# Attention's first stage rewritten across four engines: distances by TensorE, exponentials read from PSUM, splits, sums and rebases on GpSimd

## The chip, the cores and the metric

The kernel runs on one core of one Trainium2 chip. The metric is the time of one execution in microseconds (us), taken on the device; of several executions the median counts. A core has five engines with a queue of instructions each: TensorE (PE, with its weight loads listed apart as PEld), VectorE (DVE), ScalarE (ACT), GpSimd (POOL), and SyncE (SP), which issues the DMAs here. Each engine works through its queue strictly in the order written; engines wait for each other by semaphores. Lnnn is line nnn of the kernel that is shown.

## The reference

Windowed attention feeds two feed-forward blocks:

```python
# q, k, v: (2, 8, 768, 64); n_global = 8, n_local = 96
scores = (q @ k.transpose(0, 1, 3, 2)) / np.sqrt(D)
keep = is_global | is_local            # first 8 keys, or 0 <= i - j < 96
dist = np.where(is_global & ~is_local, n_local, np.abs(rel))
slopes = 2.0 ** (-8.0 * (np.arange(H) + 1) / H)      # 2^-1 .. 2^-8
scores = np.where(keep, scores - slopes[:, None, None] * dist, -1e9)
a = np.exp(scores - scores.max(-1)); a = a / (a.sum(-1) + 1e-9)
x = (a @ v) reshaped to 1536 tokens x 512
h = x @ w_in;  g = np.where(h > 0, h, np.exp(np.minimum(h, 0)) - 1);  y = g @ w_out
out = max(y @ w1, y @ w2, y @ w3) @ w_out2
```

The feed-forward weights arrive as 64-bit numbers and are turned into pairs of float32 values (a high and a low part) inside the kernel.

## The kernel before

Attention is cut into 48 steps. A step is (g, hp, t): a group g of 256 tokens, a pair hp of heads, one of the two 128-row halves t of the group. Only the keys that a row block can see are touched: 232 columns, or 128 for the first block of a sequence. Steps 0 to 15 (`first` = 16) give the first 512 tokens; they, with steps 16 and 17, make up the first stage, a loop in `windowed` that is software-pipelined by hand. The order in which the loop calls the helpers is the order of every engine's queue. The other steps are woven into the feed-forward loop `run`, one to a chunk of 128 hidden units; `run` begins when the first stage has issued its last instruction. Its first ACT instruction on a hidden chunk is L525 (`elu_exp`).

One step k in the first stage before the change:

- POOL multiplies the queries of a pair of steps by -2^(head+1)/8 (`scale_queries`, L187), once the DMA of `raw` has landed.
- PE multiplies queries and keys for two heads into two PSUM tiles (`scores_pe`, L217): S0 and S1 in even steps, y0 and y1 in odd ones.
- DVE adds the distances `rel`, scales by 2^-(head+1), writes the values `p` to SBUF and takes their minimum, in one custom instruction with an accumulator read behind it, for each of the two heads (`scores_dve`, L243).
- ACT takes exp(min - p) in place with the row sums as a by-product (`scores_act`, L264), and adds 1e-9 to the sums (`sums`, L226).
- DVE takes the reciprocal (`recip`, L255) and normalizes p (`norm`, L277, one instruction per head), both one step later.
- PE transposes p into a PSUM tile TX, y2 or y3 (`turn_pe`, L287 or L293), two steps after the scores; ACT copies that back to SBUF (`turn_act`, L304).
- PE multiplies with the values (`values_pe`, L316), three steps after the scores; ACT rounds the result to `xh` (`values_high`, L326), and DVE subtracts to get `xl` (`values_low`, L332).

From step 7 on (`CONV`) a generator `convert` puts one piece of weight conversion behind each step. For the chunks c = 0, 1, 2 these are: `c_rebase` (ACT, L404, 128x1024 values), `c_low` (DVE, L408), two `c_word` (DVE, L415, "words" from here on, each with two inputs in SBUF), `c_high` (ACT, L423) and `c_rest` (DVE, L428). In steps 0 and 1 PE also gets two idle matmuls (`fill`, L593), and eight at the start (`warm`). The distances are built once at the start from the two numbers n_global and n_local (`positions`, then `bases`, whose last instruction is L158). Before `run`, two thirds of a first feed-forward product (L505) are issued in steps 16 and 17 and at `run`'s beginning.

Of the kernel before, what the change touches and what calls it, by code (L numbers as in the profile page):

```python
# [23 lines left out]
P = 128  # L24
# [84 lines left out]
class Windowed:  # L109
# [4 lines left out]
    def __init__(self, tc, ctx, io, ps, xy, wt, act):  # L114
        self.nc, self.io, self.ps, self.xy, self.wt, self.act = tc.nc, io, ps, xy, wt, act
        self.const = ctx.enter_context(tc.tile_pool(name="acst", bufs=1))
        self.qk = ctx.enter_context(tc.tile_pool(name="qk", bufs=2))
        self.sm = ctx.enter_context(tc.tile_pool(name="sm", bufs=3))
        self.steps = [
            (g, hp, t) for g in range(NT // GRP) for hp in range(HP) for t in range(2)  # L120
        ]
        self.loaded, self.scaled = 0, set()
        self.qk_t, self.v_t = {}, {}
        self.s_t, self.p_t, self.t_t, self.at_t = {}, {}, {}, {}
        self.xraw = {}

    def positions(self, scratch):

        nc, c = self.nc, self.const
        n = P + WIN  # L130
        rel = c.tile([P, n], F32, name="rel")
        key, neg = scratch[0][:, 0:n], scratch[1][:, 0:n]
        far = 1 << 20
        o = 0
        for num, step, base, cm, kstep, kbase in (
            (P, -1, 0, 1, 1, 0),
            (PREV, -1, PREV, 1, 0, far),
            (G, 0, far, 0, 1, 0),
            (P, -1, 0, 1, 0, far),
        ):  # L140
# [8 lines left out]
        self.base, self.key, self.tmp = rel, key, neg  # L149

    def bases(self, ng, nl, a, b):
# [6 lines left out]
        nc.vector.scalar_tensor_tensor(rel, key, nl, t, op0=ALU.max, op1=ALU.min)  # L158

    def geom(self, s):  # L160

# [20 lines left out]
    def scale_queries(self, p):  # L182
        if p in self.qk_t and p not in self.scaled:
            self.scaled.add(p)
            q = self.qk_t[p][:, 0:GRP]
            c = self.steps[2 * p][1]
            self.nc.gpsimd.tensor_scalar(  # L187
                q, q, self.qsc[:, c:c + 1], 1.0, op0=ALU.mult, op1=ALU.mult
            )

    def load_values(self, k, early=False):

# [7 lines left out]
        )  # L200
        self.v_t[k], self.v_t[k + 1] = v[:, 0], v[:, 1]

    def scores_pe(self, k, tags=("S0", "S1"), m=1):

        if k >= len(self.steps):
            return
        nc = self.nc
        sp = [self.ps.tile([P, 512], F32, tag=a, name=a) for a in tags]
        for s in range(k, k + m):
            t = s % 2  # L210
            _, _, k0, n = self.geom(s)
            o = (s - k) * WIN
            for u in range(2):
                r = slice(u * D, u * D + D)
                kk = slice(GRP + k0, GRP + k0 + n)
                qk = self.qk_t[s // 2]
                nc.tensor.matmul(  # L217
                    sp[u][:, o:o + n], qk[r, t * P:t * P + P], qk[r, kk],
                    start=True, stop=True,
                )  # L220
            self.s_t[s] = [x[:, o:o + n] for x in sp]

    def sums(self, k):
        if k in self.p_t:
            m = self.p_t[k][1]
            self.nc.scalar.activation(m[:, 4:6], m[:, 2:4], AF.Copy, bias=1e-9)  # L226

    def scores_dve(self, k, early=False, other=-1):

        if k not in self.s_t:  # L230
            self.recip(other)
            return
        nc = self.nc
        i, _, _, n = self.geom(k)
        hp = self.steps[k][1]
        sp = self.s_t.pop(k)
        pool, tag = (self.act, "gh") if early and k % 4 > 1 else (self.sm, "p")
        p = pool.tile([P, 512], F32, tag=tag, name="p")
        m = self.sm.tile([P, 8], F32, tag="m", name="m", bufs=4)
        b0 = P if i else 0  # L240
        for u in range(2):
            o = slice(u * WIN, u * WIN + n)
            nc.vector.tensor_tensor_reduce(  # L243
                out=p[:, o], in0=sp[u], in1=self.base[:, b0:b0 + n],
                scale=2.0 ** -(2 * hp + u + 1), scalar=3e38,
                op0=ALU.add, op1=ALU.min, accum_out=m[:, u:u + 1],
            )
            if u == 0:
                self.recip(other)
        self.p_t[k] = p, m  # L250

    def recip(self, k):
        if k in self.p_t:
# [3 lines left out]
    def scores_act(self, k):  # L257
        if k >= len(self.steps):
            return
        n = self.geom(k)[-1]  # L260
        p, m = self.p_t[k]
        for u in range(2):
            o = slice(u * WIN, u * WIN + n)
            self.nc.scalar.activation(  # L264
                p[:, o], p[:, o], AF.Exp, bias=m[:, u:u + 1], scale=-1.0,
                accum_out=m[:, 2 + u:3 + u],
            )

# [49 lines left out]
                    start=c == 0, stop=c == nch - 1,  # L318
                )

    def values_high(self, k, x):

        if k >= 0:
            g, hp, t = self.steps[k]
            o = g * GRP + t * P
            self.nc.scalar.copy(x[0][:, hp, o:o + P], self.t_t[k][0][:, 0:P])  # L326

    def values_low(self, k, x):
        if k >= 0:
            g, hp, t = self.steps[k]  # L330
            o = g * GRP + t * P
            self.nc.vector.tensor_tensor(  # L332
                x[1][:, hp, o:o + P], self.t_t.pop(k)[0][:, 0:P],
                x[0][:, hp, o:o + P].bitcast(F32), op=ALU.subtract,
            )

    def pair_pe(self, k):

# [19 lines left out]
class Feed:  # L358
# [42 lines left out]
    def c_rebase(self, c):  # L401
        for r, _ in self.parts(c):
            a = r[..., 1].bitcast(F32)
            self.nc.scalar.activation(a, a, AF.Copy, scale=2.0 ** -112)  # L404

    def c_low(self, c):
# [442 lines left out]
def windowed(tc, ctx, io, flag):  # L849
# [3 lines left out]
    with tc.manual_schedule():  # L853
# [10 lines left out]
        x = f.split_tiles()  # L864

        def convert():
            f.c_rebase(0)
# [7 lines left out]
            f.c_rebase(1)  # L875
# [9 lines left out]
            f.c_rebase(2)  # L885
# [10 lines left out]
        h = f.ps.tile([P, 512], F32, tag="h", name="h")  # L896
        for k in range(first + 2):
            e = k % 2
            at.load_values(k, True)
            if e == 0:  # L900
                at.load_pair(k // 2 + 3, k < first)
                at.scale_queries(k // 2 + 1)
            if k <= first:
                at.scores_pe(k, (("S0", "S1"), ("y0", "y1"))[e], 1 + (k == first))
# [18 lines left out]
        at.values_pe(first - 1)  # L923
        at.turn_pe(first, "TX")
        at.values_high(first - 1, x)
        at.turn_act(first, nc.scalar.copy)
        at.values_low(first - 1, x)
        at.recip(first + 1)
        at.norm(first + 1)
        next(words, None)  # L930
        f.run(at, first + 2, x, h, lambda: covered(nc, at.const, ng, nl, flag))

# [104 lines left out]
```

## Time and profile before

| | |
|---|---|
| time, 3 runs | 570.61 us median (569.98 to 571.79) |
| span of the profiled execution | 569.0 us |
| PE busy | 549.6 us (97%) |
| DVE busy | 315.4 us (55%) |
| ACT busy | 277.1 us (49%) |
| POOL busy | 78.3 us (14%) |
| first feed-forward ACT instruction (L525), end of the first stage's path | 48.66 us |

The span runs from the first to the last instruction of the profiled execution; what a timed run has beyond it lies ahead of and behind the program (the median of the runs is 1.6 us above this span). Shares of busy time are means over stages that have different limits, so the first stage, the first 48.66 us, has to be read by itself.

### The profile page before, as it was taken

How to read it: one execution, taken by the hardware profiler on the slowest of the kernel's cores; microseconds unless marked ns; L12 is line 12 of the kernel's file. 1: busy time of each engine (PE TensorE's matmuls, PEld its weight loads, DVE VectorE, ACT ScalarE, POOL GpSimd, SP SyncE). 2: the span in 40 equal slices, each digit the busy share in tenths (PEclk: the TensorE clock that was granted, in tenths of full speed). 3: DMA queues.
4: the chain of work that ended last, by engine and by line, in shares of the span. 5: the costliest groups of instructions: out<-in, count | busy, mean ns of one | idle time of the engine just before them, and what ended most of it. 6: DMA issues, size and time to landing. Idle time of an engine off the chain costs nothing. (4 is left out here: it accounts for less than half of the span.)

```text
span 569.0 us, 7586 instructions
## 1 busy us (share of the span) xinstructions
PE 549.6 (97%) x2772; PEld 435.0 (76%) x2772; DVE 315.4 (55%) x684; ACT 277.1 (49%) x622; POOL 78.3 (14%) x87
## 2 busy tenths in 40 slices
PE   8799999999999999999999999999999999999995
PEld 6467777776777777778888888888887888888884
DVE  6987999999745333333466656567754112312112
ACT  5988777777656555554555554524323101311011
POOL 4100222222210000000011222023320000000000
PEclk9969999999999999999999999999999999999999
DMA  8919444532211111010013223122302000010002
GB/s 293 381 45 345 166 168 137 181 122 78 67 36 42 42 41 43 20 55 1 0 38 111 88 98 111 37 75 77 117 29 75 1 1 0 8 67 1 0 1 79
DMA packets 16669, 46.61 MB, mean 82 GB/s; under 512 B 1776, under 2 KB 1776, under 8 KB 16624
## 3 DMA queue, kind: packets, MB, share of 16 engines
q1 hardware_dynamic: 15760, 44.47, 22.8%
q10 hardware_dynamic: 864, 1.57, 0.8%
q8 instruction: 24, 0.39, 0.3%
q14 instruction: 21, 0.17, 0.1%
HBM read 42.90 MB, written 3.15 MB: 81 GB/s over the span
## 5 line engine op out<-in xcount | busy, mean ns | idle before, releaser
L505 PE MATMUL h<-xh,w 128*128 128x512 f32 (+1 forms) x536 | 144.5, 391 | 0.8 <-ACT xh L485 0.8
L505 PEld LDWEIGHTS h<-xh,w 128*128 128x128 f32 x536 | 98.1, 188 | 24.5 <-issue 1.8
L536 PE MATMUL y<-gh,w 128*128 128x512 f32 x384 | 98.6, 399 | 0.0
L512 ACT CAST gh<-e 128x512 fp32r<-128x512 f32 x66 | 41.0, 622 | 101.8 <-DVE e L725 87.4
L536 PEld LDWEIGHTS y<-gh,w 128*128 128x128 f32 x384 | 69.7, 188 | 18.1 <-ACT e L526 1.7
L725 DVE TENSOR_TENSOR e<-S,e 128x512 f32<-128x512 f32 x36 | 24.9, 692 | 103.5 <-PE S L505 100.8
L505 PE MATMUL h<-xl,w 128*128 128x512 f32 (+1 forms) x268 | 81.8, 386 | 0.0
L505 PE MATMUL S<-xh,w 128*128 128x512 f32 x288 | 77.0, 389 | 0.0
L530 DVE SCALAR_TENSOR_TENSOR e<-e,h 128x512 f32<-128x512 f32 x48 | 33.0, 687 | 67.7 <-ACT e L526 67.7
L505 PEld LDWEIGHTS S<-xh,w 128*128 128x128 f32 x288 | 54.1, 188 | 11.2
L525 ACT ACTIVATE e<-h 128x512 f32<-128x512 f32 x48 | 28.7, 597 | 65.2 <-PE h L505 63.0
L462 POOL TENSOR_TENSOR w<-wr,w 128x512 fp32r<-128x512 f32 x24 | 35.4, 1474 | 166.1 <-ACT w L461 166.1
L505 PEld LDWEIGHTS h<-xl,w 128*128 128x128 f32 x268 | 50.0, 188 | 10.3
L517 DVE TENSOR_TENSOR gl<-e,gh 128x512 fp32r<-128x512 f32 x50 | 39.8, 796 | 31.8 <-ACT gh L512 31.6
L264 ACT ACTIVATE p<-p,m 128x232 f32<-128x232 f32 (+1 forms) x96 | 44.8, 469 | 24.4 <-DVE m L243 24.4
L544 PE MATMUL y<-gl,w 128*128 128x512 f32 x192 | 51.5, 390 | 0.0
L415 DVE SCALAR_TENSOR_TENSOR wr<-wr 128x1024 uint32<-128x1024 uint32 (+1 forms) x36 | 49.9, 1395 | 0.8 <-ACT wr L404 0.2
L505 PE MATMUL S<-xl,w 128*128 128x512 f32 x144 | 44.3, 389 | 0.0
L451 DVE SCALAR_TENSOR_TENSOR wr<-wr 128x512 uint32<-128x512 uint32 x48 | 43.0, 896 | 2.2
L544 PEld LDWEIGHTS y<-gl,w 128*128 128x128 f32 x192 | 36.0, 188 | 7.9 <-issue 0.3
L569 PE MATMUL y<-w,gh 128*128 128x512 f32 x144 | 37.3, 390 | 0.4 <-POOLq L941 0.4
L517 POOL TENSOR_TENSOR gl<-e,gh 128x512 fp32r<-128x512 f32 x16 | 21.0, 1310 | 104.3 <-ACT gh L512 104.3
(85 smaller groups left out, 604.4 us busy)
## 6 DMA issues: line engine op xcount, KB each, us to landing
wr<-wa SPq DMA_DIRECT2D x14, 1024.0 KB, 6.4
wr<-wb SPq DMA_DIRECT2D x24, 512.0 KB, 3.3
v<-v SPq DMA_DIRECT2D x24, 256.0 KB, 2.8
raw<-qk SPq DMA_DIRECT2D x16, 312.0 KB, 3.1
raw<-qk SPq DMA_DIRECT2D x8, 260.0 KB, 3.3
wr<-wa SPq DMA_DIRECT2D x4, 512.0 KB, 3.8
out<-ot ACTq DMA_DIRECT2D x6, 256.0 KB, 2.6
out<-ot SPq DMA_DIRECT2D x6, 256.0 KB, 2.5
```

What stands on the lines that cost most here:

```text
L264: self.nc.scalar.activation(p[:, o], p[:, o], AF.Exp, bias=m[:, u:u + 1], scale=-1.0, accum_out=m[:, 2 + u:3 + u],)
L415: self.nc.vector.scalar_tensor_tensor(r[..., 0], r[..., 1], v, r[..., 0], op0=op, op1=ALU.bitwise_or)
L451: self.nc.vector.scalar_tensor_tensor(t, a, c, t, op0=op, op1=ALU.bitwise_or)
L462: nc.gpsimd.tensor_tensor(w[:, j % 2, 1], v, w[:, j % 2, 0].bitcast(F32), op=ALU.subtract)
L505: nc.tensor.matmul(out[:, o:n], w[:, part % 2, c * P:c * P + P], (xl if part == 2 else xh)[:, c, o:n], start=c == 0 and part == 0, stop=c ...
L512: self.nc.scalar.copy(gh[:, 0:n], e[:, 0:n])
L517: (engine or self.nc.vector).tensor_tensor(gl[:, 0:n], e[:, 0:n], gh[:, 0:n].bitcast(F32), op=ALU.subtract)
L525: self.nc.scalar.activation(e, h, AF.Relu, scale=-1.0)
L530: self.nc.vector.scalar_tensor_tensor(e, e, -1.0, h, op0=ALU.add, op1=ALU.max)
L536: self.nc.tensor.matmul(y[e][:, 0:n], w[:, a, e * P:e * P + P], g[0][:, 0:n], start=fc == 0 and a == 0, stop=False,)
L544: self.nc.tensor.matmul(y[e][:, 0:n], w[:, 0, e * P:e * P + P], g[1][:, 0:n], start=False, stop=fc == NFC - 1,)
L569: nc.tensor.matmul(o[r], gh[:, r * P:r * P + P], w[:, a], start=j == 0 and a == 0, stop=False,)
```

## The change

The first stage's sixteen full steps are divided anew; steps 16 and 17 keep the custom DVE instruction but get their sums from POOL too.

- The queries are scaled by -1/8 alone, and PE adds slope times distance to the scores: two more matmuls to a step, with a diagonal 128x128 matrix 2^-(head+1) as weights and the distances (`baser`, in float32r) as moving operand. ACT builds the eight diagonals at the start.
- DVE takes only the minimum, straight from PSUM (`least`); ACT reads the scores from PSUM for its exponential. The PSUM tile of a step is therefore free when ACT is done with it.
- The two halves of a pair are multiplied with the values together, at the even step k for steps k-4 and k-3. ACT copies the result to SBUF once, and POOL makes both parts of the split there. Only the last pair is split by ACT and DVE.
- 1e-9 is added to the sums by POOL, and the reciprocal moves between the two minima of the next step.
- The three rebases of weights move from ACT to POOL.

```diff
+        self.slopes = c.tile([P, H, P], F32R, name="slopes")
+        for h in range(H):
+            nc.scalar.mul(self.slopes[:, h], self.ident, 2.0 ** -(h + 1))
...
+            if early:
+                i, hp = self.geom(s)[0], self.steps[s][1]
+                b0 = P if i else 0
+                for u in range(2):
+                    nc.tensor.matmul(
+                        self.s_t[s][u], self.slopes[:, 2 * hp + u], self.baser[:, b0:b0 + n],
+                        start=False, stop=True,
+                    )
...
+            if early:
+                self.nc.gpsimd.tensor_scalar(
+                    m[:, 4:6], m[:, 2:4], 1e-9, 1.0, op0=ALU.add, op1=ALU.mult
+                )
+                return
             self.nc.scalar.activation(m[:, 4:6], m[:, 2:4], AF.Copy, bias=1e-9)
...
+    def least(self, k, other=-1):
+
+        nc = self.nc
+        m = self.sm.tile([P, 8], F32, tag="m", name="m", bufs=4)
+        for u in range(2):
+            nc.vector.tensor_reduce(m[:, u:u + 1], self.s_t[k][u], axis=AX.X, op=ALU.min)
+            if u == 0:
+                self.recip(other)
...
-                p[:, o], p[:, o], AF.Exp, bias=m[:, u:u + 1], scale=-1.0,
+                p[:, o], s[u] if s else p[:, o], AF.Exp, bias=m[:, u:u + 1], scale=-1.0,
...
+            if early:
+                self.nc.gpsimd.tensor_scalar(
+                    a, a, 2.0 ** -112, 1.0, op0=ALU.mult, op1=ALU.mult
+                )
+                continue
             self.nc.scalar.activation(a, a, AF.Copy, scale=2.0 ** -112)
...
-            at.values_pe(k - 3)
+            if e == 0:
+                at.pair_pe(k - 4)
             at.turn_pe(k - 2, ("TX", "y2", "y3")[k % 3])
...
-            at.scores_dve(k, True)
-            at.values_high(k - 3, x)
+            if early:
+                at.least(k, k - 1)
+            else:
+                at.scores_dve(k, True)
+                at.recip(k - 1)
+            if e == 0 and k >= 4:
+                g, hp, _ = at.steps[k - 4]
+                at.pair_out(k - 4, nc.scalar.copy)
+                f.split_part(x, at.xraw[g], g, hp, 1, nc.gpsimd)
             at.turn_act(k - 2, nc.scalar.copy)
             at.scores_act(k)
-            at.sums(k)
-            at.recip(k - 1)
+            at.sums(k, True)
             at.norm(k - 1)
-            at.values_low(k - 3, x)
```

In `split_part` POOL makes two instructions of a split: a multiplication by 1 that rounds to `xh` (128x256), and a subtraction from `xraw` (128x256, two inputs in SBUF).

How this stands in the queues is shown at three places. The first is POOL's queue in the first stage. Before, from the identity matrix on (raw is the tile with queries and keys, gl a feed-forward tile):

```order
masks.py:199 AFFINE_SELECT ident<-ident 128x128
L187 TENSOR_SCALAR raw<-raw,qsc 128x256 x10
L517 TENSOR_TENSOR gl<-e,gh 128x512 x2
L187 TENSOR_SCALAR raw<-raw,qsc 128x256
L517 TENSOR_TENSOR gl<-e,gh 128x512 x2
```

Now, from step 5 to step 9 of the same stage (m holds the sums, xh and xl are the split, wr is a weight chunk):

```order
L241 TENSOR_SCALAR m<-m 128x2 x2
L195 TENSOR_SCALAR raw<-raw 128x256
L510 TENSOR_SCALAR xh<-xraw 128x256
L515 TENSOR_TENSOR xl<-xraw,xh 128x256
L241 TENSOR_SCALAR m<-m 128x2 x2
L429 TENSOR_SCALAR wr<-wr 128x1024
L195 TENSOR_SCALAR raw<-raw 128x256
L510 TENSOR_SCALAR xh<-xraw 128x256
L515 TENSOR_TENSOR xl<-xraw,xh 128x256
L241 TENSOR_SCALAR m<-m 128x2 x2
```

Ten instructions that waited for nothing but DMAs became a queue in which the sums of a step stand behind a scaling, a split and, at step 8, behind the first rebase.

The second place is PE's queue in steps 4 and 5 (S and y with a number are score tiles or the tiles that take transposes and values; v are the values). Before:

```order
L217 MATMUL S_238<-raw 128x128
L217 MATMUL S_239<-raw 128x128
L316 MATMUL TX<-p,v 64x128 x4
L287 MATMUL y_246<-ident,p 128x128 x2
L217 MATMUL y_262<-raw 128x232
L217 MATMUL y_263<-raw 128x232
L316 MATMUL y_246<-p,v 64x128 x2
L293 MATMUL y_268<-ident,p 116x128 x4
```

Now, the same two steps:

```order
L223 MATMUL S_252<-raw 128x128
L223 MATMUL S_253<-raw 128x128
L232 MATMUL S_252<-baser,slopes 128x128
L232 MATMUL S_253<-baser,slopes 128x128
L347 MATMUL TX<-p,v 64x128 x6
L318 MATMUL y_264<-ident,p 128x128 x2
L223 MATMUL y_282<-raw 128x232
L223 MATMUL y_283<-raw 128x232
L232 MATMUL y_282<-baser,slopes 128x232
L232 MATMUL y_283<-baser,slopes 128x232
L324 MATMUL y_288<-ident,p 116x128 x4
```

Four matmuls were added to the pair of steps, and the values of both halves stand together in the even one.

The third place is DVE's queue at step 8, with what each instruction waits for (wr is the weight chunk of a word). Before:

```order
L243 ISA p,m<-S_348,rel 128x232 [waits PE_49]
L243 ISA m 128x1
L243 ISA p,m<-S_349,rel 128x232 [waits PE_49]
L243 ISA m 128x1
L255 RECIPROCAL m<-m 128x2 [waits Activation_49]
L277 TENSOR_SCALAR p<-p,m 128x232 [waits DVE_49]
L277 TENSOR_SCALAR p<-p,m 128x232
L332 TENSOR_TENSOR xl<-y_323,xh 128x128 [waits Activation_49]
L415 SCALAR_TENSOR_TENSOR wr<-wr 128x1024
```

Now:

```order
L276 TENSOR_REDUCE m<-S_369 128x1 [waits PE_49]
L285 RECIPROCAL m<-m 128x2 [waits Pool_49]
L276 TENSOR_REDUCE m<-S_370 128x1 [waits PE_49]
L308 TENSOR_SCALAR p<-p,m 128x232 [waits DVE_49,Activation_49]
L308 TENSOR_SCALAR p<-p,m 128x232 [waits Activation_49]
L444 SCALAR_TENSOR_TENSOR wr<-wr 128x1024 [waits Pool_49]
```

The subtraction is gone, the reciprocal and the word wait for POOL, and the second minimum stands behind the reciprocal.

## Rows read from the trace of the kernel before

**Rows 1.** The page: span.

```profile
span 569.0 us, 7586 instructions
```

**Rows 2.** Timeline of ACT: start, duration; the first feed-forward instruction.

```profile
48.66 0.60 ACT L525 ACTIVATE e<-h 128x512 f32<-128x512 f32 x1 [0.84 <-PE h L505]
```

**Rows 3.** Windows: stretch, busy time and instructions of each engine, granted clock, DMA.

```profile
4.69:17.59 12.90, 11.71 (x87) 7.36 (x86) 11.07 (x59) 10.07 (x45) 2.98 (x5) 1.00 1.03 381
17.59:30.33 12.74, 8.68 (x75) 5.21 (x74) 12.12 (x44) 12.05 (x40) 2.58 (x4) 1.00 0.84 324
30.33:39.96 9.63, 9.63 (x50) 5.78 (x49) 8.71 (x34) 7.24 (x24) 0.00 (x0) 0.50 0.16 62
39.96:48.66 8.70, 8.02 (x71) 6.60 (x71) 7.56 (x24) 7.17 (x24) 0.00 (x0) 0.97 0.57 208
```

**Rows 4.** Timeline of DVE: one step of the first stage, and a c_low.

```profile
22.09 0.38 DVE L243 CUSTOM_DVE_ANT_0 p<-y,rel 128x232 f32<-128x232 f32 x1
...
22.73 0.15 DVE L255 RECIPROCAL m<-m 128x2 f32<-128x2 f32 x1
22.91 0.59 DVE L277 TENSOR_SCALAR p<-p,m 128x232 f32<-128x232 f32 x2
23.42 0.28 DVE L332 TENSOR_TENSOR xl<-y,xh 128x128 fp32r<-128x128 f32 x1
23.62 1.22 DVE L415 SCALAR_TENSOR_TENSOR wr<-wr 128x1024 uint32<-128x1024 uint32 x1
24.75 0.39 DVE L243 CUSTOM_DVE_ANT_0 p<-S,rel 128x232 f32<-128x232 f32 x1
...
26.29 0.69 DVE L408 TENSOR_SCALAR wr<-wr 128x1024 uint32<-128x1024 uint32 x1
```

**Rows 5.** Timeline of the start: the last distance on DVE, PE's scores and fills.

```profile
4.70 0.80 PE L217 MATMUL S<-raw 64*128 64x128 f32 x4
...
5.42 1.18 PE L593 MATMUL z<-ident 128*128 128x128 f32 x4
...
6.15 0.61 DVE L158 SCALAR_TENSOR_TENSOR rel<-sc,nf 128x360 f32<-128x360 f32 x1
...
7.13 0.71 PE L593 MATMUL z<-ident 128*128 128x128 f32 x4
...
8.94 0.52 PE L287 MATMUL y<-ident,p 128*128 128x128 f32 x2 [0.68 <-DVE p L277]
```

**Rows 6.** Timeline of PE: scores of steps 2, 4, 5 and 6, values in between.

```profile
7.77 0.49 PE L217 MATMUL S<-raw 64*128 64x128 f32 x4
...
10.98 0.49 PE L217 MATMUL S<-raw 64*128 64x128 f32 x4
11.73 0.66 PE L316 MATMUL TX<-p,v 116*64 116x128 f32 x8 [0.25 <-ACT p L304]
...
12.68 0.66 PE L217 MATMUL y<-raw 64*128 64x232 f32 x4
...
14.29 0.49 PE L217 MATMUL S<-raw 64*128 64x128 f32 x4
```

**Rows 7.** Timeline of PE: scores at the lower clock, step 16, a float32r product.

```profile
33.64 1.14 PE L217 MATMUL S<-raw 64*128 64x232 f32 x4
...
39.96 1.33 PE L217 MATMUL S<-raw 64*128 64x232 f32 x8
41.22 0.97 PE L505 MATMUL h<-xh,w 128*128 128x256 f32 x6
```

**Rows 8.** POOL's scaling, by tile: count, duration in ns (min/median/max).

```profile
L187 POOL TENSOR_SCALAR raw<-raw,qsc x11: 477/562/1454, 4.0 to 59.2; 128x256 f32<-128x256 f32 x11
```

**Rows 9.** Timeline, 57.9 to 60.7 us: a word of DVE between two POOL instructions.

```profile
57.94 1.29 POOL L517 TENSOR_TENSOR gl<-e,gh 128x512 fp32r<-128x512 f32 x1 [5.27 <-ACT gh L512]
...
58.36 1.95 DVE L415 SCALAR_TENSOR_TENSOR wr<-wr 128x1024 uint32<-128x1024 uint32 x1
...
59.20 1.45 POOL L187 TENSOR_SCALAR raw<-raw,qsc 128x256 f32<-128x256 f32 x1
```

More of the change, by code (lines that the diff above doesn't have):

```diff
@@ L122, in __init__ @@
         self.loaded, self.scaled = 0, set()
+        self.first = BLOCKS[0] // GRP * 8
         self.qk_t, self.v_t = {}, {}
@@ L157, in bases @@
         nc.vector.tensor_tensor(t, t, rel, op=ALU.max)
-        nc.vector.scalar_tensor_tensor(rel, key, nl, t, op0=ALU.max, op1=ALU.min)
+        nc.vector.scalar_tensor_tensor(
+            self.baser[:, a:b], key, nl, t, op0=ALU.max, op1=ALU.min
+        )
     def geom(self, s):
@@ L186, in scale_queries @@
             c = self.steps[2 * p][1]
-            self.nc.gpsimd.tensor_scalar(
-                q, q, self.qsc[:, c:c + 1], 1.0, op0=ALU.mult, op1=ALU.mult
-            )
+            v = self.qsc[:, c:c + 1] if 2 * p >= self.first else -(D ** -0.5)
+            self.nc.gpsimd.tensor_scalar(q, q, v, 1.0, op0=ALU.mult, op1=ALU.mult)
     def load_values(self, k, early=False):
@@ L201, in load_values, with scores_pe @@
         self.v_t[k], self.v_t[k + 1] = v[:, 0], v[:, 1]
-    def scores_pe(self, k, tags=("S0", "S1"), m=1):
+    def scores_pe(self, k, tags=("S0", "S1"), m=1, early=False):
         if k >= len(self.steps):
@@ L218, in scores_pe, with sums @@
                     sp[u][:, o:o + n], qk[r, t * P:t * P + P], qk[r, kk],
-                    start=True, stop=True,
+                    start=True, stop=not early,
                 )
             self.s_t[s] = [x[:, o:o + n] for x in sp]
-    def sums(self, k):
+            if early:
[6 more added lines that the diff above has]
+                    )
+    def sums(self, k, early=False):
         if k in self.p_t:
             m = self.p_t[k][1]
+            if early:
[3 more added lines that the diff above has]
+                return
             self.nc.scalar.activation(m[:, 4:6], m[:, 2:4], AF.Copy, bias=1e-9)
@@ L243, in scores_dve @@
             nc.vector.tensor_tensor_reduce(
-                out=p[:, o], in0=sp[u], in1=self.base[:, b0:b0 + n],
+                out=p[:, o], in0=sp[u], in1=self.baser[:, b0:b0 + n].bitcast(F32),
                 scale=2.0 ** -(2 * hp + u + 1), scalar=3e38,
@@ L250, in scores_dve @@
         self.p_t[k] = p, m
+    def least(self, k, other=-1):
[5 more added lines that the diff above has]
+                self.recip(other)
+        pool, tag = (self.act, "gh") if k % 4 > 1 else (self.sm, "p")
+        self.p_t[k] = pool.tile([P, 512], F32, tag=tag, name="p"), m
     def recip(self, k):
@@ L261, in scores_act @@
         p, m = self.p_t[k]
+        s = self.s_t.pop(k, None)
         for u in range(2):
@@ L319, in values_pe, with pair_split @@
                 )
[L321 to L335, printed above, removed]
+    def pair_split(self, k, x):
+        g, hp, _ = self.steps[k]
+        o = (slice(None), hp, slice(g * GRP, g * GRP + GRP))
+        self.t_t.pop(k)
+        t = self.t_t.pop(k + 1)[0][:, 0:GRP]
+        self.nc.scalar.copy(x[0][o], t)
+        self.nc.vector.tensor_tensor(x[1][o], t, x[0][o].bitcast(F32), op=ALU.subtract)
     def pair_pe(self, k):
@@ L399, in parts, with c_rebase @@
         return [(self.wraw[j], j % 2) for j in (2 * c, 2 * c + 1) if j in self.wraw and c < NFC]
-    def c_rebase(self, c):
+    def c_rebase(self, c, early=False):
         for r, _ in self.parts(c):
             a = r[..., 1].bitcast(F32)
+            if early:
+                self.nc.gpsimd.tensor_scalar(
+                    a, a, 2.0 ** -112, 1.0, op0=ALU.mult, op1=ALU.mult
+                )
+                continue
             self.nc.scalar.activation(a, a, AF.Copy, scale=2.0 ** -112)
@@ L866, in convert @@
         def convert():
-            f.c_rebase(0)
+            f.c_rebase(0, True)
             f.c_low(0)
@@ L874, in convert @@
             f.c_high(0)
-            f.c_rebase(1)
+            f.c_rebase(1, True)
             f.c_low(1)
@@ L884, in convert @@
             f.c_high(1)
-            f.c_rebase(2)
+            f.c_rebase(2, True)
             f.c_low(2)
@@ L898, in windowed @@
             e = k % 2
+            early = k < first
             at.load_values(k, True)
             if e == 0:
-                at.load_pair(k // 2 + 3, k < first)
+                at.load_pair(k // 2 + 3, early)
                 at.scale_queries(k // 2 + 1)
             if k <= first:
-                at.scores_pe(k, (("S0", "S1"), ("y0", "y1"))[e], 1 + (k == first))
+                at.scores_pe(k, (("S0", "S1"), ("y0", "y1"))[e], 1 + (k == first), early)
             if k >= first:
                 f.product(h, f.w[0][:, 0], x, GRP, 0, (k - first) * 6, 6)
-            at.values_pe(k - 3)
+            if e == 0:
+                at.pair_pe(k - 4)
             at.turn_pe(k - 2, ("TX", "y2", "y3")[k % 3])
@@ L922, in windowed @@
                 f.w_load()
-        at.values_pe(first - 1)
+        at.pair_pe(first - 2)
         at.turn_pe(first, "TX")
-        at.values_high(first - 1, x)
+        at.pair_split(first - 2, x)
         at.turn_act(first, nc.scalar.copy)
-        at.values_low(first - 1, x)
         at.recip(first + 1)
         at.norm(first + 1)
+        for g in range(first // 8):
+            at.take(g)
         next(words, None)
```

1 line of the change is left out of this document (added).

## The prediction

> **What bounds the kernel now.** I first read the page and its slices, to see that the change touches only the first stage of a span of 569.0 us [rows 1]. Then I looked for the end of that stage: ACT's first feed-forward instruction, at 48.66 us, which had waited for PE's product [rows 2]. Whatever moves this start moves the rest, since the feed-forward loop behind it is fed in the same order. So the forecast is the shift of 48.66. The windows cut the stage into four stretches, at PE's scores of step 0 (4.69), step 8 (17.59) and step 16 (39.96), the middle also at 30.33, where the clock falls [rows 3]. The reader should see that no single engine bounds it. Up to step 8 PE is busy 11.71 us of 12.90, and ACT, which begins late, nearly all the time. From 17.59 to 30.33 DVE (12.12 of 12.74) and ACT (12.05) are both full. [...]
>
> DVE's timeline gives the price of a step with a word, by starts: two custom instructions 0.64, reciprocal 0.18, two norms 0.51, subtraction 0.20, word 1.13, together 2.66 us [rows 4].
>
> **The change, stretch by stretch.**
>
> *Start, steps 0 to 3.* The distance matmul of step 0 needs the last distance, which DVE finishes at 6.76 [rows 5]. Before, PE ran ahead in that time: fill and scores of step 1 stood in 5.42 to 7.13. Now both are queued behind the waiting matmul. A distance matmul costs (0.97 - 0.29)/5 = 0.136 us from start to start, like a float32r product of 256 columns (0.29 is the end of the last of the six) [rows 7]; two to a step are 0.27. It could cost somewhat less, with 128 or 232 columns, and not nothing, as PE has it in sequence. From 6.80 on: distances 0.27, fill 0.64 (7.13 to 7.77), scores 0.66, distances 0.27, fill 0.64 puts the scores of step 2 at 9.28 instead of 7.77 [rows 5, 6], 1.5 us late. PE then had 0.68 us of waiting [rows 5], which absorbs that much; the distances of steps 2 and 3 (0.54) give some back. I take **+1.0**, bounds 0.8 and 1.4. ACT's eight diagonals hide ahead of 6.8, since its first exponential needs the first distance anyway; uncovered they would cost eight short ACT instructions once, near 2 us.
>
> *Steps 4 to 7.* A pair of steps took 3.31 us (10.98 to 14.29), 0.25 of it PE's wait for ACT [rows 6]. PE's own work becomes 3.31 - 0.25 + 0.54 = 3.60. ACT is relieved of sums and casts, but PE, not ACT, then sets the pace. With 0.1 for a split that meets a norm, two pairs are **+0.8**; bounds 0.4 and 1.2.
>
> *Steps 8 to 15.* Before: 12.74 + 9.63 = 22.37 us. DVE's step loses its subtraction (0.20). The minimum from PSUM replaces custom instruction and accumulator read; this trace has no such reduction. The custom instruction streams the same 232 columns of PSUM in 0.32 from start to start, and the subtraction 128 columns in 0.20 [rows 4], so 0.28 to 0.34 each; I take 0.32, no gain. Six steps with a word or c_rest at 2.46 and two with c_low at 2.66 - 0.20 - 1.13 + 0.69 = 2.02 make 18.8 us. PE's work fits under that at the higher clock; ACT has lost sums, casts and rebases.
>
> [...]
>
> What is added is POOL: for each pair a scaling of 0.48 [rows 8], a rounding of the same shape, 0.48, and a subtraction with two inputs, half of the 1.29 for twice the columns [rows 9], 0.65. That is 1.6 a pair, 6.4 in this stretch. A rebase has four times the columns of a scaling: at most 1.9 us, less if part of 0.48 is fixed; I take 1.7, bounds 1.5 and 1.9. Two of them are 3.4. In all 9.8 us. The question is whether it lies beside DVE's work, and the trace answers it. POOL's subtraction started at 57.94 and ended at 59.23; DVE's word, issued at 58.36, took 1.95 us instead of 1.22, so that its 1.22 began when POOL ended. POOL's scaling, issued at 59.20, then took 1.45 instead of 0.48: it ran when the word was over [rows 9]. The two exclude each other. The custom instruction, which reads one SBUF operand, and the reciprocal show no such stretching.
>
> [...]
>
> So 9.8 us of POOL can hide only beside minima and reciprocals, 0.82 a step, 6.6 us. Were all of it used, the stretch would take 18.8 + 9.8 - 6.6 = 22.0; were none, 28.6. I take 22.5, near the lower end, because ACT's copy of a pair and the exponentials release POOL when DVE's minima come up. That is **+0.1**. At step 8 this is tightest: the first rebase, a scaling, and a split stand ahead of the sums on POOL, and on DVE the second minimum and the norms stand behind the reciprocal that waits for those sums; behind them are PE's transposition and ACT's copy. The sums themselves, 128x2 on POOL instead of ACT, I take at no difference: POOL's short hop replaces ACT's, and below nothing speaks only that ACT's queue is shorter.
>
> *From step 16 to the end of the stage.* Before 8.70 us [rows 3]. The third rebase (1.7) starts behind c_low and meets the norms of step 14 after 0.82 of minima and reciprocal: 0.9 is exposed. One more scaling and split (1.6) lie between c_rest, two words and the norms, with 0.2 exposed. The pair split by ACT and DVE costs about what two single ones did. **+1.1**; bounds 0 and 3.3.
>
> The sum: 1.0 + 0.8 + 0.1 + 1.1 = **+3.0 us**: the stage ends near 51.7, the span is 572.0. The median of the timed runs lies 1.6 us over the profiled span, so I forecast **573.6 us**. DMAs keep their order, and their landings lie ahead of their use by more than this; the loop behind is not changed.
>
> **Rivals.**
>
> *POOL's work costs DVE next to nothing* (22 in 100). The splits find their gaps, or a small POOL instruction does not hold DVE up as the wide one in rows 9 did. Then the middle takes 18.8 (-3.6), the end +0, the start still +1.8: -1.8, **568.8 us**, faster. [...] Against it: rows 9. The mechanism decides from 1.8 us: I have 3.7 (22.5 - 18.8) and 1.1 of exposed POOL time; under 1.8 in all, the change gains.
>
> *Half of it* (18 in 100): exposed POOL time near 1.8, with gains and losses even: **570.6 us**, within 0.3% of before, about what a measurement of this kernel can tell from none.
>
> *The clock* (20 in 100). Fills took 1.18 us at 5.42 and 0.71 at 7.13 [rows 5]: PE runs slower at first, and was kept busy without a gap until it got faster. Now it stands still from about 5.5 to 6.8. If it gets its speed later, two fills (0.94), a score (0.48) and distances (0.3) add 1.7: 575.3. [...] For it: the fall before came after a stretch in which PE had gaps. Against: PE has more to do now.
>
> **How the numbers follow.** 40 in 100 for the forecast as told, with its own range of 572.3 to 575.2 (the bounds of start and pairs, and 22.0 to 23.5 in the middle). The range of 568.4 to 577.0 takes in the faster rival just, and the clock's; a middle near 28.6 is outside. Chances: the faster rival is faster, 0.22; half of it is the same, 0.18; the forecast and the clock are slower, 0.60.
>
> **What would show it.** In the new profile: scores of step 2 near 9.3, of step 8 near 19.4, of step 16 near 42, and L525's successor near 51.7. Norms and words longer than 0.34 and 1.22 wherever a rebase or split runs, and splits longer than 0.48 and 0.65. A granted clock of 1.00 throughout. The prediction is wrong if words keep 1.22 beside POOL's rebases, if the reduction from PSUM is far from 0.32, or if PE's clock behaves otherwise.

## The result, and the profile after

The changed kernel took 578.54 us in the median of 20 runs (570.95 to 582.13), the kernel before 570.98 in 20 runs beside them (568.58 to 576.33). The ratio is 1.0073, 95% interval 1.0044 to 1.0102, formed without the longest runs of either kernel: slower by about 0.7%. The median of all runs lies 1.3% above that of before, and above my range's upper end of 577.0; the profiled execution took 574.19 us, 0.6 from the forecast. The difference is in the runs themselves. Seven lie at 570.95 to 574.19, thirteen at 577.28 to 582.13; of before, sixteen lie at 568.58 to 572.77 and four at 574.16 to 576.33.

The page of the changed kernel, the span and its granted clock in 40 slices, answers to [rows 1]:

```profile
span 572.1 us, 7648 instructions
PEclk7999999999999999999999999999999999999999
```

ACT's first feed-forward instruction, by its timeline, answers to [rows 2]:

```profile
51.70 0.60 ACT L554 ACTIVATE e<-h 128x512 f32<-128x512 f32 x1 [0.83 <-PE h L534]
```

It stands at the predicted 51.7, 3.04 us behind the 48.66 of before, and all behind it has shifted by as much (572.1 - 51.70 = 520.4, before 520.3). But the way there is another than I wrote. The windows of the changed kernel, cut at scores of step 0 (4.61), step 8 (21.60), 31.88 and step 16 (42.32), answer to [rows 3]:

```profile
4.61:21.60 16.99, 15.16 (x99) 10.64 (x98) 10.09 (x39) 9.85 (x41) 5.08 (x14) 0.80 0.96 358
21.60:31.88 10.28, 8.21 (x64) 5.03 (x63) 9.22 (x23) 7.45 (x23) 7.32 (x13) 1.00 0.84 292
31.88:42.32 10.44, 8.91 (x74) 5.67 (x73) 10.44 (x25) 7.98 (x24) 8.22 (x12) 1.00 0.20 59
42.32:51.70 9.38, 8.26 (x77) 6.58 (x76) 9.13 (x27) 5.97 (x19) 5.93 (x8) 1.00 0.57 209
```

Before, the low clock stood in the middle (0.50 from 30.33 to 39.96). Now it stands at the start (0.80 in the mean to 21.60), and the middle has 1.00. PE's timeline of the start answers to [rows 5, 6]:

```profile
4.61 0.49 PE L223 MATMUL S<-raw 64*128 64x128 f32 x4
6.94 0.41 PE L232 MATMUL S<-baser,slopes 128*128 128x128 f32 x2 [1.83 <-DVE baser L163]
7.18 0.66 PE L622 MATMUL z<-ident 128*128 128x128 f32 x4
7.77 1.08 PE L223 MATMUL y<-raw 64*128 64x232 f32 x4
...
10.37 0.80 PE L223 MATMUL S<-raw 64*128 64x128 f32 x4
...
14.78 0.49 PE L223 MATMUL S<-raw 64*128 64x128 f32 x4
```

PE was at its higher clock at 4.61 already (scores of 128 columns 0.49, as in [rows 6]). Then it stood still for 1.83 us in front of the first distance; scores of step 1 took 1.08 instead of 0.66, those of step 2 0.80 instead of 0.49. Not before 14.78 are they at 0.49 again, and by then 3.8 us are lost (10.98 before).

### The profile page after: what moved, and what is told of

Its sections match the earlier page's. It is cut to its first block, busy times and chain, and to the rows that moved or that the text cites. A ratio compares the mean times of both kernels' runs of the same rounds, so it can differ in the third digit from the quotient of the medians.

```text
span 572.1 us, 7648 instructions
## 1 busy us (share of the span) xinstructions
PE 552.4 (97%) x2804; PEld 438.2 (77%) x2804; DVE 314.7 (55%) x637; ACT 272.2 (48%) x601; POOL 99.2 (17%) x122
## 3 DMA queue, kind: packets, MB, share of 16 engines
q1 hardware_dynamic: 15760, 44.47, 22.5%
## 5 line engine op out<-in xcount | busy, mean ns | idle before, releaser
L295 ACT ACTIVATE p<-p,m 128x232 f32<-128x232 f32 (+1 forms) x64 | 30.1, 471 | 19.2 <-DVE m L262 19.2
```

Of the source, the lines that this page charges most:

```text
L295: self.nc.scalar.activation(p[:, o], s[u] if s else p[:, o], AF.Exp, bias=m[:, u:u + 1], scale=-1.0, accum_out=m[:, 2 + u:3 + u],)
```

## Experiments

Eleven kernels; each has a profiled execution and, but for one, 12 runs (rebases back on ACT alone: 6). The ratio is to runs of the kernel before taken beside them. "First" is the start of ACT's first feed-forward instruction in the profiled execution.

| kernel | first | median (all runs) | ratio to before, interval |
|---|---|---|---|
| before | 48.66 | 570.25 to 570.98 | |
| changed | 51.70 | 578.54 (570.95 to 582.13) | 1.0073, 1.0044 to 1.0102 |
| 1 rebases on ACT | 55.63 | 578.31 (574.08 to 579.98) | 1.0124, 1.0073 to 1.0175 |
| 2 splits on ACT and DVE | 53.96 | 575.97 (568.22 to 579.38) | 1.0004, 0.9958 to 1.0050 |
| 3 fills ahead of distances | 55.96 | 571.38 (570.59 to 580.19) | 1.0030, 0.9988 to 1.0071 |
| 4 distances alone | 59.92 | 577.32 (570.37 to 583.60) | 1.0077, 1.0038 to 1.0117 |
| 5 scores ahead | 48.31 | 570.98 (570.01 to 579.17) | 1.0010, 0.9972 to 1.0048 |
| 6 before, no fills | 53.68 | 575.40 (573.93 to 576.35) | 1.0068, 1.0037 to 1.0100 |
| 7 scores ahead, splits on ACT and DVE | 46.35 | 568.45 (567.94 to 568.92) | 0.9956, 0.9926 to 0.9985 |
| 8 scores ahead, rebases on ACT | 48.42 | 571.32 (570.08 to 578.82) | 0.9999, 0.9963 to 1.0035 |
| 9 before, fills in the middle | 47.25 | 569.54 (568.51 to 575.09) | 1.0008, 0.9977 to 1.0039 |
| 10 as 7, rebases on ACT | 46.74 | 568.94 (568.48 to 577.25) | 0.9974, 0.9946 to 1.0001 |
| 11 as 10, sums on ACT | 47.40 | 569.65 (569.07 to 580.40) | 0.9994, 0.9966 to 1.0023 |

**1 to 4: parts undone, the start as changed.** Rebases on ACT:

```diff
-            f.c_rebase(0, True)
+            f.c_rebase(0)
```

and likewise for 1 and 2.

> The changed kernel with the three rebases of the first stage back on ACT; all else as changed. Theory 1 (POOL and DVE exclude each other): in the changed kernel the norms beside the three rebases took 0.78, 0.82 and 0.81 us instead of 0.33, together 1.4 us on a DVE that is full there. Without the rebases on POOL these norms take 0.33 to 0.48, and ACT's first feed-forward instruction stands near 50.3 instead of 51.70. Theory 2 (ACT's queue is the dearer place): three rebases of about 1.15 us on ACT hold up exponentials and copies, and the instruction stands at 51.7 or up to 1 us later. A difference of 1.4 us is 0.25% of the time.

Splits on ACT and DVE:

```diff
-                g, hp, _ = at.steps[k - 4]
-                at.pair_out(k - 4, nc.scalar.copy)
-                f.split_part(x, at.xraw[g], g, hp, 1, nc.gpsimd)
+                at.pair_split(k - 4, x)
...
-        for g in range(first // 8):
-            at.take(g)
```

(`take` drops the tile that ACT copies into for POOL; it isn't made here.)

> The changed kernel with the split of the values of a pair back on ACT (rounding from PSUM) and DVE (subtraction from PSUM); POOL keeps scalings, sums and rebases. Theory 1 (POOL and DVE exclude each other): the lengthening of norms and words beside POOL's splits was about 2.2 us in steps 8 to 15 and 0.5 behind them; in its place come five subtractions of 0.41 us on DVE. So ACT's first feed-forward instruction stands about 0.6 us earlier, near 51.1. Theory 2 (a split on POOL hides for the most part): the subtractions are added to a full DVE, and the instruction stands 1 to 1.6 us later, near 53.

Fills ahead: the fill of steps 0 and 1 is called between a step's scores and its distances.

```diff
+                if k < FILL[0] and ahead:
+                    ahead()
                 i, hp = self.geom(s)[0], self.steps[s][1]
...
+                at.scores_pe(k, (("S0", "S1"), ("y0", "y1"))[e], 1 + (k == first), early,
+                             lambda: f.fill(at.ident, FILL[1]))
...
-            if k < FILL[0]:
-                f.fill(at.ident, FILL[1])
```

> The changed kernel with the fill matmuls of steps 0 and 1 ahead of the distance matmuls of the same step instead of behind the step's transpositions. Theory 1 (the clock): in the changed kernel PE stood still from 5.1 to 6.94 us, and its granted clock was 0.50 from about 7.8 to 14.6. With the fills in that gap PE stands still for less than 1 us, scores of step 2 start near 8.7 instead of 10.37, those of step 8 near 19.4 instead of 21.60, the granted clock is 1.00 from about 7 us on, and the first feed-forward instruction comes about 2 us earlier, near 49.7, unless the clock falls later. The runs should scatter less, with fewer near 578. Theory 2 (the wait for the last distance is what costs): PE's order behind the distance changes by the 0.64 us of one fill only, and step 8 starts at 20.9 or later at the same clock.

Distances alone: the edits of rebases and splits together, and

```diff
-            at.sums(k, True)
+            at.sums(k)
```

> The changed kernel with sums and rebases back on ACT and the split of the values on ACT and DVE: only the distances on PE, the minimum from PSUM and the exponential from PSUM are left of the change; POOL has scalings alone. Theory 1 (POOL and DVE exclude each other, and the price of the change in the middle is POOL's): norms and words take 0.33 and 1.22 throughout but beside scalings; steps 8 to 15 take about 19 us instead of 20.7, and the first feed-forward instruction stands near 49.7. Theory 2 (ACT was the bound that POOL's work relieves): ACT has 4.6 us of rebases and sums more, is full as before the change, and the instruction stands at 52 to 53.

None of the four could be read by its end: what they were to differ by, 0.6 to 2 us, drowned in the clock. In all four profiled executions the first instruction came 2.3 to 8.2 us later than in the changed kernel, whatever had been undone. The windows of the run with rebases on ACT show why:

```profile
5.00:10.00 5.00, 3.44 (x22) 2.64 (x22) 3.29 (x11) 2.30 (x11) 0.76 (x2) 0.83 1.04 372
10.00:15.00 5.00, 5.00 (x23) 3.31 (x23) 2.22 (x11) 1.99 (x9) 0.79 (x3) 0.50 1.03 410
15.00:20.00 5.00, 5.00 (x28) 3.64 (x26) 1.78 (x8) 2.28 (x10) 1.91 (x5) 0.50 0.69 230
20.00:25.00 5.00, 5.00 (x27) 3.10 (x25) 1.68 (x8) 2.93 (x11) 1.72 (x4) 0.50 0.69 247
25.00:30.00 5.00, 5.00 (x30) 3.48 (x30) 3.67 (x12) 3.12 (x8) 0.95 (x4) 0.62 0.23 87
```

PE had stood still for 1.56 us in front of the first distance, and then had 0.50 until about 29 us (0.62 in the mean of the last row), busy without a gap, while DVE and ACT waited for it. In the changed kernel's own profiled execution the same phase ended at 14.6 (a granted clock of 0.51 from 7.80 to 14.60). That the two groups of its runs are the shorter and the longer of such phases is inferred from these traces; none of its own longer runs has one. With fills ahead PE still stood still for 1.02 us; eight of those 12 runs lie at 570.59 to 571.60 and four at 578.78 to 580.19, the profiled one among the four. Four long runs of 12 against thirteen of 20 hint that less standing still makes the longer phase rarer, and don't show it; neither theory's number was met.

One thing can be read in them whatever the clock is. Here are the third rebase and DVE's neighbours of it, in the changed kernel's timelines of DVE and POOL, and then DVE's of the run with rebases on ACT, behind a c_low too:

```profile
42.80 0.37 DVE L276 TENSOR_REDUCE m<-y 128x1 f32<-128x232 f32 x1
43.10 1.05 DVE L308 TENSOR_SCALAR p<-p,m 128x232 f32<-128x232 f32 x2
...
42.63 1.15 POOL L429 TENSOR_SCALAR wr<-wr 128x1024 f32<-128x1024 f32 x1
```

```profile
36.71 0.37 DVE L276 TENSOR_REDUCE m<-y 128x1 f32<-128x232 f32 x1
37.01 0.57 DVE L308 TENSOR_SCALAR p<-p,m 128x232 f32<-128x232 f32 x2
```

Two norms take 1.05 beside a rebase and 0.57 without. The second norm starts just behind the end of the rebase (43.78), and the minimum, which ran beside the rebase, is not lengthened.

**5 and 6: PE's order at the start, by itself.** The changed kernel with scores of step 1 and a fill ahead of the first distance, as before the change:

```diff
+            if k == 0:
+                at.scores_pe(0, ("S0", "S1"), 1, True)
+                f.fill(at.ident, FILL[1])
+                at.scores_pe(1, ("y0", "y1"), 1, True)
+            if k < 2:
+                at.distance(k)
-            if k <= first:
+            elif k <= first:
...
-            if k < FILL[0]:
+            if k == 1:
                 f.fill(at.ident, FILL[1])
```

(distance(k) is the loop of distance matmuls, taken out of scores_pe for steps 0 and 1.)

> The changed kernel with PE's order of the first two steps written as before the change: scores of step 0, a fill, scores of step 1, and only then the distance matmuls of steps 0 and 1. Nothing is left out. Theory 1 (the clock, and PE's standing still in front of the first distance as what decides it): PE has work from 4.7 to 7 us, the granted clock is 1.00 from 7 us on, scores of step 2 start near 8.7, those of step 8 near 19.4, ACT's first feed-forward instruction near 49.7, and nearly all runs lie in one group near 570 to 572, none or few near 578. Theory 2 (PE's 0.27 us of distances a step and the wait for the last distance cost the time, whatever the clock does): the runs scatter as those of the changed kernel do, 571 to 582, with a median of 576 or more.

And the kernel before without the two lines that fill in steps 0 and 1:

> The kernel before the change without its fill matmuls of steps 0 and 1; nothing else is left out, the outputs don't depend on them. Theory 1 (standing still costs the clock): PE has gaps between 5.5 and 9 us, the granted clock is 0.50 for some 6 to 20 us behind them in most runs, the steps 2 to 8 take up to twice as long, and a good part of the runs lies 4 to 9 us above 570, as those of the changed kernel do. Theory 2 (the lower clock of the changed kernel has another cause, such as the added matmuls): the time stays within 2 us of 570.

Both went as the clock's theory has it. With scores ahead, PE's timeline shows 0.67 us of standing still in place of 1.83, and scores and distances keep their shorter times:

```profile
5.64 0.66 PE L223 MATMUL y<-raw 64*128 64x232 f32 x4
6.98 0.41 PE L235 MATMUL S<-baser,slopes 128*128 128x128 f32 x2 [0.67 <-DVE baser L163]
7.23 0.44 PE L235 MATMUL y<-baser,slopes 128*128 128x232 f32 x2
...
9.92 0.66 PE L223 MATMUL y<-raw 64*128 64x232 f32 x4
```

Step 8 starts at 18.21 (before 17.59, changed 21.60), step 16 at 38.92, and ACT's first instruction at

```profile
48.31 0.60 ACT L557 ACTIVATE e<-h 128x512 f32<-128x512 f32 x1 [0.85 <-PE h L537]
```

Ten of the 12 runs lie at 570.01 to 571.29, two at 578.62 and 579.17. So of the changed kernel's 3.04 us in the profiled execution more than all (3.39), and of its 7.6 us in the median 7.0 (578.54 is 7.56 above the kernel before beside it, 570.98 here is 0.53 above), is the order of PE's first instructions. The mirror image holds in the time: the kernel before, without its fills, is at 573.93 to 576.35 in all 12 runs. PE stood still for 1.14 and 0.66 us between 6 and 9, and its timeline reads, near the end of the slow phase:

```profile
7.41 0.96 PE L217 MATMUL S<-raw 64*128 64x128 f32 x4 [1.14 <-DVE m L243]
...
28.17 1.14 PE L217 MATMUL S<-raw 64*128 64x232 f32 x4
29.25 1.12 PE L316 MATMUL TX<-p,v 116*64 116x128 f32 x8
30.30 0.92 PE L293 MATMUL y<-ident,p 128*116 128x128 f32 x4
31.14 0.66 PE L217 MATMUL y<-raw 64*128 64x232 f32 x4
```

Up to 29 us scores of 232 columns take 1.14 as at the lower clock of [rows 7]; at 31.14 they take 0.66. None of the scores before that has its shorter time either (128 columns 0.80 at 4.70, against 0.49; 232 columns 0.98 at 5.28 and 1.15 at 9.65, against 0.66). By these rows PE didn't lose its speed in this execution, as it did in the changed kernel's; it had not got it yet, which was my rival *clock*. The theory's granted clock of 0.50 isn't there: the record reads 1.00 up to 32 us.

**7 and 8: the parts again, the clock now quiet.** The edits of 2 and 1 on top of 5.

> The run with scores ahead of the distances, and in addition the split of a pair's values on ACT (rounding from PSUM) and DVE (subtraction from PSUM) instead of POOL. Against the run with scores ahead alone, theory 1 (POOL's splits hold up DVE by more than the subtractions cost): first feed-forward instruction about 0.6 us earlier, and 0.5 us off the time. Theory 2: the subtractions of 0.41 us each come on top, 1 to 1.6 us later.

> The run with scores ahead of the distances, and in addition the three rebases on ACT instead of POOL. Against the run with scores ahead alone, theory 1 (each rebase on POOL lengthens a norm on DVE by 0.48 us): 1.0 to 1.4 us earlier at the first feed-forward instruction and in the time, norms at 0.33 us where the rebases were. Theory 2 (on ACT a rebase of 1.15 us holds up exponentials and copies that DVE and PE wait for): no gain, or up to 1 us later.

Without POOL's splits it is 1.96 us earlier (46.35), and 2.5 in the median. That is the faster kernel of the study: all 12 runs at 567.94 to 568.92, below before by 0.4%. Theory 1 holds, and the gain is larger than its 0.6. DVE's groups by line from step 8 to 16 show where it comes from, first with POOL's splits (run 5), then without (run 7); the last columns are busy time and mean duration in ns:

```profile
L311 DVE TENSOR_SCALAR p<-p,m 128x232 f32<-128x232 f32 x14 | 7.1, 544 | 0.0
L447 DVE SCALAR_TENSOR_TENSOR wr<-wr 128x1024 uint32<-128x1024 uint32 x4 | 5.1, 1264 | 0.0
...
L288 DVE RECIPROCAL m<-m 128x2 f32<-128x2 f32 x8 | 1.2, 154 | 1.1 <-POOL m L244 1.1
```

```profile
L311 DVE TENSOR_SCALAR p<-p,m 128x232 f32<-128x232 f32 x14 | 4.9, 387 | 0.0
L447 DVE SCALAR_TENSOR_TENSOR wr<-wr 128x1024 uint32<-128x1024 uint32 x4 | 4.8, 1211 | 0.0
L362 DVE TENSOR_TENSOR xl<-y,xh 128x256 fp32r<-128x256 f32 x3 | 1.2, 412 | 0.0
...
L288 DVE RECIPROCAL m<-m 128x2 f32<-128x2 f32 x8 | 1.2, 152 | 0.3 <-POOL m L244 0.2
```

Without the splits the norms take 2.2 us less and the words 0.3, the reciprocals wait 0.8 less for POOL's sums, and the four subtractions cost 1.6 (three of 0.41 and one on another tile). That is 1.7 of the 1.8 us by which the stretch is shorter (20.71 to 18.87).

The rebases are the other way about. Their norms do shrink, but the end doesn't come earlier (48.42 against 48.31), nor the median (571.32 against 570.98). Theory 2's place is seen from 29.50 to 33.00, where PE's granted clock was 0.57 in this execution, after a stretch with 3.17 of 4.50 us busy:

```profile
25.00:29.50 4.50, 3.17 (x19) 1.66 (x17) 4.50 (x13) 3.87 (x9) 3.20 (x5) 1.00 0.71 278
29.50:33.00 3.50, 3.06 (x22) 2.39 (x22) 3.45 (x8) 1.67 (x7) 1.21 (x3) 0.57 0.04 7
```

**9 to 11: the middle, and the parts that are left.** The kernel before with its fill in steps 7 to 13 too:

```diff
-            if k < FILL[0]:
+            if k < FILL[0] or 7 <= k < 14:
                 f.fill(at.ident, FILL[1])
```

> The kernel before the change with the two fill matmuls of steps 0 and 1 also in steps 7 to 13; nothing is left out. In the changed kernel PE's granted clock stayed at 1.00 where it was 0.50 before (30 to 40 us), and steps 8 to 15 took 20.7 us instead of 22.4. Theory 1 (that gain is the clock, held because PE has more to do): with fills in its gaps the clock stays at 1.00 here too, DVE sets the pace with six steps of 2.66 and two of 2.22 us, 20.4 in all, and the first feed-forward instruction comes up to 2 us earlier than 48.66, near 46.7. Theory 2 (the gain is DVE's, from minima that are cheaper than custom instructions with their accumulator reads and from the subtractions it lost): the fills, some 0.45 us each step, are added to PE or hide, and steps 8 to 15 take 22.4 or more.

Run 7 with rebases on ACT (the edit of 1), and that with sums on ACT (the last edit of 4):

> The run with scores ahead and the split on ACT and DVE, and in addition the three rebases on ACT: of POOL's new work only the sums are left. Theory 1 (each rebase on POOL costs DVE 0.48 us): steps 8 to 15 take about 17.9 us instead of 18.87, the first feed-forward instruction stands near 45.0 instead of 46.35, and the time is near 567.2. Theory 2 (PE gets gaps while ACT does the rebases between 20 and 30 us, and its clock falls, as in the run with scores ahead and rebases on ACT): a stretch of some 3 us at 0.50, PE's steps 2 us longer there, and 569 to 571.

> The run before in this list with the sums on ACT too: POOL has no new work, and only the distances on PE with minimum and exponential from PSUM are left of the change, with PE's order of the first two steps as before it. Theory 1 (the sums on POOL gain nothing, since they end behind DVE's word, as a sum on ACT would): within 0.5 us of the run with sums on POOL. Theory 2 (ACT is short of time, and sixteen sums of 0.2 us come on top): 1 to 3 us later at the first feed-forward instruction, and PE's clock falls between 25 and 40 us.

The fills hold the clock, as theory 1 has it. Windows of the kernel before with them, at step 8 and step 16:

```profile
18.28:37.67 19.39, 16.68 (x148) 11.53 (x147) 18.92 (x67) 17.61 (x59) 2.36 (x4) 1.00 0.62 229
```

19.39 us at 1.00 instead of 22.37, less even than the 20.4 expected; 0.7 of the 3.0 was paid ahead, as step 8 starts at 18.28 instead of 17.59. From step 16 on it took 9.58 us instead of 8.70, so that the first instruction stands only 1.41 earlier. The median is 0.8 lower, but three of the 12 runs are at 573.39 to 575.09, and the ratio's interval takes in 1.

With rebases on ACT in run 7's company the end is 0.39 later and the median 0.5 higher: theory 1 falls again, this time at a clock of 1.00, so theory 2's fall of the clock isn't the reason either. ACT's timeline shows the place, a rounding of 1.16 and a rebase of 1.13 in a row in front of a copy and the exponentials:

```profile
27.00 1.16 ACT L455 CAST w<-wr 128x1024 fp32r<-128x1024 f32 x1
28.06 1.13 ACT L436 ACTIVATE wr<-wr 128x1024 f32<-128x1024 f32 x1
29.09 0.58 ACT L338 COPY p<-y 116x512 f32<-116x512 f32 x1
29.55 0.47 ACT L298 ACTIVATE p<-y,m 128x232 f32<-128x232 f32 x1
```

Run 7 has that copy at 27.89. The sums on ACT cost 0.66 more, and 0.7 in the median: between its two theories, nearer to the first.

## Why the prediction was right, and where not

Slower was right, 573.6 is near the profiled execution's 574.19, and 51.7 was hit. That was luck, twice. The sum came out because its errors cancel: the start was 2.8 us too cheap, the three other terms together 2.75 too dear. And the profiled execution is one of the seven shorter runs of 20; the median, which I had forecast, lies 4.9 us above 573.6. The likeliest case was not the one that happened: that was the rival *clock*, at the start, and with it my own sign of being wrong, "if PE's clock behaves otherwise". (The bounds that I named for my own range add up to 572.5 to 575.4, not 572.3 to 575.2.)

| term | forecast | changed kernel | with scores ahead |
|---|---|---|---|
| start, to step 4 | +1.0 | +3.8 | +0.4 |
| steps 4 to 7 | +0.8 | +0.2 | +0.2 |
| steps 8 to 15 | +0.1 | -1.65 | -1.66 |
| from step 16 | +1.1 | +0.7 | +0.7 |
| sum | +3.0 | +3.0 | -0.35 |

*Start.* The step that failed. I priced the wait for the last distance and what is queued behind it (+1.0, bounds 0.8 and 1.4), saw in [rows 5] that the kernel before kept PE busy there until it got faster, and still left the clock to a rival of 20 in 100 and 1.7 us. "A granted clock of 1.00 throughout" and scores of step 2 near 9.3 (10.37) and of step 8 near 19.4 (21.60) fell with it. With run 5's order, in which PE stands still for 0.67 us and not 1.83, the term is +0.4. The rival's price was too small as well: it let PE get faster one step later, whereas PE had its speed at 4.61 and lost it again, and the phase lasted to 14.6 us, or to some 26 to 35 in the profiled executions of runs 1 to 4.

*Steps 4 to 7.* A pair takes 3.41 us (14.78, 18.19, 21.60), not 3.60: mis-sized by 0.19 a pair.

*Steps 8 to 15.* I forecast 22.5 us, 18.8 of DVE and 3.7 of POOL's work; it took 20.7. PE at 1.00 is not what was missed: the 18.8 took it for granted. It is what brings the stretch under the 22.37 of before, of which 9.63 are at a granted clock of 0.50. Run 9 shows that the kernel before takes 19.39 when PE is given more to do, so at one and the same clock the changed kernel's middle is 1.3 us longer, not 1.65 shorter, and run 7's (18.87) 0.5 shorter. Run 11, which keeps the distances, the minimum and the exponential from PSUM, has 1.00 there without fills and takes 19.52. What was mis-sized is DVE. A step with a word is 2.31 us and not 2.46, as the next start follows a minimum after 0.29 to 0.32 and the reciprocal after 0.07 to 0.08; and three c_lows begin in the stretch, before the change too, not two. At these prices eight steps make some 16.9 us and not 18.8. A minimum's own duration is 0.37 to 0.39 here; what the full DVE pays for it is the time until the next start, the 0.29 to 0.32, close to the 0.32 that I took. POOL's exposed time was sized about right: I took 3.7, and the norms show 14 x (0.544 - 0.336) = 2.9, the words 0.2 and the reciprocals' wait for the sums 1.1. A rebase takes 1.11 to 1.16, outside my bounds of 1.5 and 1.9.

*POOL excludes DVE* is shown for norms by 1.05 and 0.57, and by runs 5 and 7 (a norm of 128x232 0.544 and 0.387 in the mean, a word 1.264 and 1.211). It goes both ways: POOL's sums of 128x2 take 0.19 us alone and up to 1.24 beside DVE's wide instructions (at 36.45, beside the c_rest of 36.43 to 37.64). That POOL's 9.8 us hide only beside minima and reciprocals, 6.6 us in my forecast of the middle, rested on rows of a word alone, and no run shows the 6.6; what the runs show in its place are the 2.9, 0.2 and 1.1 us above, by which POOL held up the norms, the words and the reciprocals. For norms and c_low the kernel before has it too: two norms of 0.79 beside a scaling, where those in [rows 4] take 0.59, and a scaling of 0.93 instead of 0.48, issued in the c_low of 26.29:

```profile
9.71 0.48 POOL L187 TENSOR_SCALAR raw<-raw,qsc 128x256 f32<-128x256 f32 x1 [0.98 <-DMA raw<-qk]
...
9.78 0.79 DVE L277 TENSOR_SCALAR p<-p,m 128x232 f32<-128x232 f32 x2
...
26.39 0.93 POOL L187 TENSOR_SCALAR raw<-raw,qsc 128x256 f32<-128x256 f32 x1 [1.02 <-DMA raw<-qk]
```

What I had wrong is which of POOL's work pays. At a quiet clock, each step by the runs' first instructions (and medians): distances alone 47.40 (569.65); sums on POOL -0.66 (-0.7); rebases on POOL -0.39 (-0.5), as 0.48 of DVE is less than 1.13 of ACT in front of the exponentials (read from the traces of runs 7 and 10, not tested by itself); splits on POOL +1.96 (+2.5); the order of the start +3.39 (+7.0). The first two steps are under 0.15% of the time and rest on one profiled execution each, with the medians on their side. Two parts gain, one loses, and PE's order outweighs all.

*From step 16.* 9.38 instead of 8.70, +0.7 in place of 1.1; the rebase exposes 0.48 and not 0.9.

What stays open is when a slow phase comes and how long it lasts: to 14.6 us in one execution, to 26 to 35 in others. The length of the gap alone doesn't decide it. In run 3 a gap of 1.02 us in front of the first distance, from 5.80 to 6.82, was followed by 0.50; in run 9 PE stood still for 0.97 us ahead of 9.23, and its scores kept their 0.66:

```profile
9.23 0.52 PE L287 MATMUL y<-ident,p 128*128 128x128 f32 x2 [0.97 <-DVE p L277]
9.68 0.66 PE L217 MATMUL y<-raw 64*128 64x232 f32 x4
```

The point at which PE gets its speed differs too, and with it the gap. Run 7 has run 5's order, and the same instructions up to step 4, but PE was slower at first there (scores of step 0 0.80, in run 5 0.49), was still busy when the last distance came, and didn't stand still in front of it:

```profile
4.70 0.80 PE L223 MATMUL S<-raw 64*128 64x128 f32 x4
...
6.37 0.66 PE L223 MATMUL y<-raw 64*128 64x232 f32 x4
6.96 0.44 PE L235 MATMUL S<-baser,slopes 128*128 128x128 f32 x2
```

Why run 5 had two long runs of 12 and run 7 none is not shown. Nor are the changed kernel's long runs all of the kind that I traced. Seven of the thirteen have a mean granted clock of 0.976 to 0.982, as the profiled executions of runs 1 to 3 have (0.980 to 0.983), against 0.991 to 0.997 in the seven shorter runs; the other six read 0.992 to 1.000. Run 6 has both readings at one and the same time (575.65 us at 0.997, 575.71 at 0.977), so those six may be runs in which PE got its speed late; no trace of one was kept.

## What to carry to other kernels

Before a matmul that waits for something is put into PE's queue, look at what it keeps from running: here 0.24 us of distances (6.94 to 7.18 in the changed kernel), queued ahead of work that could have run while their operand was late, cost 7.0 us in the median, and the same matmuls two places further down 0.4 us at the start. When a stretch is compared across a change, ask first at which clock each of the two ran, and test the parts only once that is the same; a total that agrees says nothing of its terms. Work goes to POOL if it is short or stands where the other engine's queue is dearer, and not beside a full DVE just because POOL is free: here the sums gained 0.66 us there and the rebases 0.39, and the splits cost 1.96.

## What the runs showed of the hardware that was not expected

- PE standing still for 1.0 to 2.1 us near 5 to 7 us of the span was followed by a granted clock of 0.50 for 7 to some 27 us (the changed kernel and runs 1 to 4), although PE was then busy without a gap (the run with rebases on ACT: 5.00 of 5.00 us in three slices at 0.50).
- The granted clock doesn't show every slow phase: the kernel before without fills reads 1.00 from 5 to 30 us, while its scores take 1.14 us until 29 and 0.66 from 31.14. The durations of a known shape tell.
- PE's filling work can gain time: with fills of 0.54 us a step (30.69 to 31.23 in run 9) PE had 1.00 where it had 0.50, and steps 8 to 15 of the kernel before took 3.0 us less.
